# A two-layer decode kernel on one core: hand-written phases against a list scheduler, one pool of ten load slots, a fifth kept V pair and a searched load order

## The chip, the cores and the metric

The kernel runs on one core of a Trainium2 chip. The metric is the device time of one execution in microseconds (us); lower is better. Engines are named as in the profile: PE does matmuls, PEld its weight loads, DVE is the vector engine, ACT does exponentials and copies, SP issues the loads (SPq is its queue). L426 is line 426 of the kernel.

## The reference, cut to what matters

Two layers run one after the other, with the same weights and the same cache. Each is attention of one new token per batch over a cache of 8192 positions, then a gated FFN.

```python
# B=4, Hq=32, Hkv=8, Sk=8192, Dh=128, D=512, F=1792, all bf16
def _A_ref(x, k_cache, v_cache, wq, wo):
    q = (x @ wq) ...                                   # 4 query heads share one K/V head
    scores = einsum("bhqd,bhkd->bhqk", q, k) * Dh ** -0.5
    o = einsum("bhqk,bhkd->bhqd", softmax(scores), v)
    return o ... @ wo

x = x + _A_ref(_layernorm(x), ...)                     # layer 0
x = x + _B_ref(_layernorm(x), ...)                     # silu(x @ w_gate) * (x @ w_up) @ w_down
x = x + _A_ref(_layernorm(x), ...)                     # layer 1: the same K and V again
x = x + _B_ref(_layernorm(x), ...)
```

K and V are 67 MB each, and each layer streams them (the kernel before reads 265.56 MB from HBM for both layers, weights included). One load ("pair") is 1024 KB, called 1 MB here: half the positions of one K or V head. There are 128 K pairs and 128 V pairs in the two layers. A few V pairs of each batch are kept from layer 0 for layer 1 and are loaded only once.

A batch goes from layer 0 to layer 1 alone. In between lies its *chain*: output projection, LayerNorm, FFN, LayerNorm, query projection. The chain is made of many small steps that depend on each other and move no K or V.

## The kernel before: the parts that matter

The order of all work is written by hand as phases. Small steps are put on a list `delayed` and come out one by one after K or V units; at the end of a phase they are all run out (`settle`).

```python
NRING = 10                    # ring of ten 0.5 MB buffers, used strictly in turn
NRET = 8                      # eight 0.5 MB buffers reserved for kept V
TAIL1 = [14, 10, 6]; NFILL = [16, 16, 14, 12]; LATE = [12, 12, 16]; FL = [1, 2, 1, 1, 2, 3, 2, 2]  # tuned by hand
...
def do(u):                    # one K or V unit of 0.5 MB
    if u[0] == "k":
        k_front(u)            # DVE transpose
        ...                   # QK matmuls of the pair before: flush()
    else:
        flush(); v_unit(u)    # 16 P.V matmuls
    run_delayed(); pump()     # small steps; then issue every load whose buffer is free

def settle():
    for _ in range(5):
        run_delayed(True)     # all softmax steps at once, one after the other
...
elif name == "C1":            # the chain of batch b, with FL[i] units between its steps
    hold["on"] = True
    add_to_x(x0T, "x0", OPJ)
    some(FL[0]); ln_center(); some(FL[1]); ffn_gate(); ln_scale()
    ...
```

## Time and profile before

| | before |
|---|---|
| time, median of 3 runs | 704.52 us (703.98 to 706.74) |
| span of the profiled run | 703.3 us |
| read from HBM | 265.56 MB in 240 pair loads and the weights |
| PE, DVE busy | 468.5 us, 380.7 us |

The page of the kernel before, parts 1 to 3: busy time and share of the span, then the DMA engines' busy share in tenths and the GB/s in 40 slices of 17.6 us, then the bytes.

```profile
PE 468.5 (67%) x10564; PEld 275.8 (39%) x10564; DVE 380.7 (54%) x586; ACT 48.6 (7%) x114; POOL 0.7 (0%) x6
...
GB/s 359 375 402 407 285 414 418 420 401 417 412 319 409 420 316 424 397 420 371 360 409 420 397 414 388 410 419 380 301 358 423 410 345 422 386 319 404 404 372 58
...
HBM read 265.56 MB, written 0.00 MB: 378 GB/s over the span
```

No engine is busy all the time. The load stream runs at about 420 GB/s in its good slices (416 to 426 in the undisturbed stretches of 10 us), and dips elsewhere. At 420 GB/s the bytes alone take 265.56 / 0.42 = 632.3 us. The other 71.0 us of the span are start, end and dips. I call this difference, span less bytes at 420 GB/s, the *shortfall*. It is an estimate made from the span and the bytes, and it serves to compare kernels.

The stretches table of the kernel before (stretch in us; length; busy us and count on PE, PEld, DVE, ACT, POOL; granted PE clock; DMA share; GB/s):

```profile
70.00:80.00 10.00, 3.85 (x21) 2.63 (x21) 4.34 (x12) 2.45 (x5) 0.00 (x0) 0.50 0.91 348
80.00:90.00 10.00, 9.26 (x191) 4.02 (x191) 7.06 (x8) 0.00 (x0) 0.00 (x0) 0.50 0.69 247
...
250.00:260.00 10.00, 7.73 (x163) 4.05 (x162) 7.42 (x8) 0.00 (x0) 0.00 (x0) 0.50 0.77 288
...
490.00:500.00 10.00, 5.13 (x147) 4.91 (x147) 1.45 (x9) 0.50 (x2) 0.00 (x0) 0.50 0.82 298
500.00:510.00 10.00, 8.04 (x177) 4.24 (x185) 7.56 (x10) 0.00 (x0) 0.00 (x0) 0.50 0.78 281
```

The dip at 70 to 90 us is the first softmax; 490 to 510 us is a chain. The timeline of DVE at the first softmax of the kernel before (start, length, engine, line, operation, tiles, count; in brackets the idle time before and who ended it, where "issue" means that the engine waited for nothing the profile shows) shows why loading stops:

```profile
62.37 2.37 DVE L412 STREAM_TRANSPOSE ring<-ring 128x1024 uint32<-128x1024 uint32 x2 [0.26 <-DMA ring<-in_A_k_cache_dram]
66.52 2.48 DVE L443 TENSOR_REDUCE negm<-ps 128x1 f32<-128x512 f32 x4 [1.79 <-PE ps L426]
...
72.87 0.24 DVE L500 TENSOR_SCALAR selw<-selL,gl 128x32 f32<-128x32 f32 x1
77.67 0.36 DVE L510 RECIPROCAL invL<-ps 128x32 f32<-128x32 f32 x1 [4.55 <-PE ps L508]
77.94 9.07 DVE L412 STREAM_TRANSPOSE ring<-ring 128x1024 uint32<-128x1024 uint32 x8
```

From 64.7 to 77.9 us DVE transposes no K. In DVE's program the transposes stand behind the last softmax step, for which DVE sits idle 4.55 us; eight follow at once when it is done. No K is consumed, no buffer comes free, and the loading queue stops: in the timeline of SP the load issued at 66.56 us is followed by the next only at 82.31.

```profile
66.56 6.46 SPq L92 DMA_DIRECT2D ring<-in_A_k_cache_dram  x1
82.31 0.33 SPq L92 DMA_DIRECT2D ring<-in_A_v_cache_dram  x1
```

SP's own waits, in total, count and longest, before:

```profile
SPq L62 <- PE ps L426: 329.6, 120, 19.5
SPq L62 <- PE ps L522: 213.1, 89, 11.5
```

L426 are the QK matmuls and L522 the P·V matmuls. SP waits for them because they free the buffers.

### The profile page before, as it was taken

Reading aid. Unit: us, or ns where it says so; the run is one execution under the profiler, and the core shown is the slowest. Engines: PE = TensorE matmul, PEld = TensorE weight load, DVE = VectorE, ACT = ScalarE, POOL = GpSimd, SP = SyncE. Lnnn points to the kernel's source line nnn. Section 1 sums busy time; section 2 is a strip of 40 time slices with the busy share of each in tenths; the row PEclk is TensorE's granted clock in tenths of the full one; section 3 lists DMA queues with packets and bytes.
Section 4 is the critical chain, followed back from the end, with each engine's and each line's share of the span. In section 5 each row is a group of like instructions: output and inputs, shape, how many; then the busy total and the mean of one; then the engine's idle time right before and its main releaser. Section 6 shows DMA issues by size and latency. Waiting matters only on the chain.

```text
span 703.3 us, 22406 instructions
## 1 busy us (share of the span) xinstructions
PE 468.5 (67%) x10564; PEld 275.8 (39%) x10564; DVE 380.7 (54%) x586; ACT 48.6 (7%) x114; POOL 0.7 (0%) x6
## 2 busy tenths in 40 slices
PE   2565656565676577867756678677786676586676
PEld 2111323245642233347522443246432376532375
DVE  4977654540288857741576557652566610289501
ACT  1001100020000110020000200011000110000200
POOL 0000000000000000000000000000000000000000
PEclk9955555555567755555586555655555555567555
DMA  8999799999989989999999999999899999989991
GB/s 359 375 402 407 285 414 418 420 401 417 412 319 409 420 316 424 397 420 371 360 409 420 397 414 388 410 419 380 301 358 423 410 345 422 386 319 404 404 372 58
DMA packets 42268, 267.00 MB, mean 380 GB/s; under 512 B 4024, under 2 KB 9920, under 8 KB 10944
## 3 DMA queue, kind: packets, MB, share of 16 engines
q1 hardware_dynamic: 42176, 265.58, 94.2%
q8 instruction: 82, 1.34, 0.7%
q14 instruction: 10, 0.08, 0.0%
HBM read 265.56 MB, written 0.00 MB: 378 GB/s over the span
## 4 chain that ended last, share of the span: by engine, by line
PE 34%; DMA 31%; DVE 27%; issue 5%; ACT 3%; SPq 1%
DMA ring<-in_A_k_cache_dram 21%; DVE ring L412 21%; PE ps L426 11%; PE ps L522 10%; DMA ring<-in_A_v_cache_dram 8%; DVE negm L443 3%; PE ps L588 3%; PE ps L642 2%; PE ps L489 2%; ACT pp L492 2%; DMA wq_sb<-in_A_wq_dram 2%; PE ps L547 2%; PE ps L678 1%; PE ps L564 1%; DVE pp L480 1%
## 5 line engine op out<-in xcount | busy, mean ns | idle before, releaser
L426 PE MATMUL ps<-ring,qpad 32*32 32x512 bf16 x4096 | 253.5, 566 | 121.3 <-DVE ring L412 120.7
L412 DVE STREAM_TRANSPOSE ring<-ring 128x1024 uint32<-128x1024 uint32 x256 | 299.0, 1217 | 47.9 <-DMA ring<-in_A_k_cache_dram 43.8
L426 PEld LDWEIGHTS ps<-ring,qpad 32*32 32x32 bf16 x4096 | 70.0, 111 | 270.1 <-DVE ring L412 208.7
L522 PE MATMUL ps<-pp,ring 128*128 128x4 bf16 x3072 | 96.3, 166 | 24.3 <-issue 14.3
L522 PEld LDWEIGHTS ps<-pp,ring 128*128 128x128 bf16 x3072 | 92.9, 104 | 44.5 <-issue 32.6
L531 DVE TENSOR_TENSOR oT<-ps,invL 128x4 bf16<-128x4 f32 x64 | 10.7, 167 | 141.0 <-PE ps L522 140.9
L445 ACT ACTIVATE pp<-ps,negm 128x512 bf16<-128x512 f32 x32 | 21.6, 686 | 451.9 <-DVE negm L443 451.9
L522 PE MATMUL ps<-pp,kept 128*128 128x4 bf16 x1024 | 31.8, 166 | 6.9 <-DMA kept<-in_A_v_cache_dram 5.2
L522 PEld LDWEIGHTS ps<-pp,kept 128*128 128x128 bf16 x1024 | 30.1, 104 | 15.4 <-issue 9.6
L443 DVE TENSOR_REDUCE negm<-ps 128x1 f32<-128x512 f32 x32 | 19.9, 682 | 15.1 <-PE ps L426 15.1
L547 PE MATMUL ps<-oT,wo_sb 128*128 128x4 bf16 x640 | 21.5, 166 | 5.0 <-issue 3.3
L588 PE MATMUL ps<-xnT,wq_sb 128*128 128x4 bf16 x640 | 18.7, 166 | 6.8 <-issue 4.5
L489 PE MATMUL ps<-ident,pp 128*128 128x128 bf16 x128 | 16.5, 310 | 9.8 <-ACT pp L492 6.4
L547 PEld LDWEIGHTS ps<-oT,wo_sb 128*128 128x128 bf16 x640 | 20.1, 105 | 6.6 <-issue 4.4
L588 PEld LDWEIGHTS ps<-xnT,wq_sb 128*128 128x128 bf16 x640 | 17.9, 104 | 8.8 <-issue 6.3
L492 ACT ACTIVATE pp<-ps 128x1024 bf16<-128x1024 bf16 x16 | 16.4, 1024 | 32.8 <-PE ps L489 32.8
L463 PE MATMUL ps<-identf,gm 128*1 128x128 f32 x8 | 2.6, 320 | 22.4 <-DVE gm L455 22.4
L489 PEld LDWEIGHTS ps<-ident,pp 128*128 128x128 bf16 x128 | 12.3, 141 | 11.1 <-ACT pp L492 7.4
L567 DVE TENSOR_REDUCE var<-ps 128x4 f32<-128x16 f32 x10 | 1.7, 174 | 25.5 <-PE ps L564 25.5
L580 ACT ACTIVATE lnv<-var,eps_sb 128x4 f32<-128x4 f32 x10 | 3.0, 298 | 153.3 <-DVE var L567 153.3
L510 DVE RECIPROCAL invL<-ps 128x32 f32<-128x32 f32 x8 | 2.9, 357 | 19.1 <-PE ps L508 19.1
L678 PE MATMUL ps<-hT,wd_sb 128*128 128x4 bf16 x280 | 8.5, 166 | 6.0 <-issue 4.7
(68 smaller groups left out, 151.9 us busy)
## 6 DMA issues: line engine op xcount, KB each, us to landing
ring<-in_A_k_cache_dram SPq DMA_DIRECT2D x128, 1024.0 KB, 8.3
ring<-in_A_v_cache_dram SPq DMA_DIRECT2D x96, 1024.0 KB, 9.0
kept<-in_A_v_cache_dram SPq DMA_DIRECT2D x16, 1024.0 KB, 12.8
wq_sb<-in_A_wq_dram SPq DMA_DIRECT2D x1, 4096.0 KB, 12.3
wo_sb<-in_A_wo_dram SPq DMA_DIRECT2D x4, 1024.0 KB, 13.6
wg_sb<-in_B_w_gate_dram SPq DMA_DIRECT2D x2, 896.0 KB, 10.9
wu_sb<-in_B_w_up_dram SPq DMA_DIRECT2D x2, 896.0 KB, 12.2
wd_sb<-in_B_w_down_dram SPq DMA_DIRECT2D x2, 896.0 KB, 15.2
```

What stands on the lines that cost most here:

```text
L412: T.op("dve", lambda e: e.transpose(v, v), reads=[key], writes=[key])
L426: T.op("pe", lambda e: e.matmul(ps[32 * c:32 * (c + 1), a * BW:(a + 1) * BW], lhsT=qp[rows, es_, g, :], rhs=kt[n][rows, :, es_ // 2, :, es ...
L443: T.op("dve", lambda e: e.tensor_reduce(negm[:, q, a:a + 1], bank(a), AX.X, ALU.max, negate=True), reads=[f"pb{a}"], writes=[f"negm{q}_{a}"])
L445: T.op("act", lambda e: e.activation(pblk(q)[:, :, a, :], bank(a).rearrange("p (t j) -> p t j", j=32), ACTF.Exp, bias=negm[:, q, a:a + 1], ...
L489: T.op("pe", lambda e: e.matmul(stg[:, t * P:(t + 1) * P], lhsT=pp[:, q, blk * P:(blk + 1) * P], rhs=ident[:], is_transpose=True, start=Tr ...
L492: T.op("act", lambda e: e.activation(pp[:, q, f * 1024:(f + 1) * 1024], stg[:, :], ACTF.Copy), reads=[f"pb{bk}"], writes=[f"pp{q}_{a}" for ...
L522: T.op("pe", lambda e: e.matmul(ps[:, bk * BW:bk * BW + REP], lhsT=ap[:, t * Dh:(t + 1) * Dh], rhs=pp[:, q, col:col + REP], start=(c == 0 ...
L531: T.op("dve", lambda e: e.tensor_tensor(oT[:, l, g * REP:(g + 1) * REP, b], ps[:, bk * BW:bk * BW + REP], invL[:, q, g * REP:(g + 1) * REP ...
L547: T.op("pe", lambda e: e.matmul(ps[:, OPJ * BW + nq * B:OPJ * BW + (nq + 1) * B], lhsT=wo_sb[:, h, nq * P:(nq + 1) * P], rhs=oT[:, l, h, : ...
L588: T.op("pe", lambda e: e.matmul(misc[:, h * B:(h + 1) * B], lhsT=wq_sb[:, kt, h * Dh:(h + 1) * Dh], rhs=xnT[:, kt * B:(kt + 1) * B], start ...
L642: T.op("pe", lambda e: e.matmul(ps[:, bk * BW + fo * B:bk * BW + (fo + 1) * B], lhsT=w_sb[:, kt, fo * P:(fo + 1) * P], rhs=xnT[:, kt * B:( ...
L678: T.op("pe", lambda e: e.matmul(misc[:, nq * B:(nq + 1) * B], lhsT=wd_sb[:, fo, nq * P:(nq + 1) * P], rhs=hT[:, fo * B:(fo + 1) * B], star ...
```

## The change

The intent: describe the whole program as steps with an engine, a time and dependences; let a list scheduler place all of them and all loads at build time; and issue each engine's instructions in the planned order. The buffers become one pool of ten 1 MB slots, in which kept V simply hold their slot longer. Five pairs per batch are kept instead of eight half pairs (the same as four pairs). The order of the loads is a string found by a search. The step times are written in the code.

```diff
+class Plan:
+    HOP = 0.2
+    LOAD_LEAD = 0.8
+    LOAD_TAIL = 1.4
+    ...
+    def run(self):          # earliest start first; among ready steps, the lowest prio
+        ...
+                    slots.sort()
+                    f, i = slots[0]          # a load takes the slot that comes free first
+        ...
+    def emit(self):
+        for s in sorted(self.steps + self.loads, key=lambda s: (s.start, s.prio[0])):
+            s.fn()
+
+ORDER = ("KKKqKVKKKoKKKgKKKKVKVVKKKgKuKKVoKVVVKKKVKKKVV..."   # cut: K, V pairs and weights
+KEPT = [5, 5, 5, 5]
+NSLOT = 10
...
-        ring = sb("ring", [P, NRING, NB * Dh], BF16)
-        kept = sb("kept", [P, NRET, NB * Dh], BF16)
+        pool = sb("pool", [P, NSLOT, 2 * UE], BF16)
...
+        CHAIN = [-10.0]                       # softmax and chain steps go first when ready
+                tr.append(PL.add("dve", 1.22, t, [ld], prio))            # K transpose
+            st = PL.add("pe", 1.95, qk, tr + [qd, prev] + ..., prio)     # QK of one pair
+                st = PL.add("pe", 1.0, pv, [prev, p_ready[(l, b)], lds.get(u)], prios[i], ...)
+            return PL.add("pe", 0.03 * KT * len(heads), mm, deps, CHAIN, take=tag)   # query projection
...
-        phases = [("A1", 0, A_of(0, 0, range(NCH // 2)))]
-        ...                                   # cut: phases, delayed, settle, hold
+        PL.run()
+        PL.emit()
```

The room for the tenth slot comes mostly from smaller query buffers. Work on the engines is otherwise the same, apart from a query spread of 16 small matmuls where 4 stood.

## The prediction

> **What bounds it now.** The load stream. The page counts 265.6 MB read from HBM in 703.3 us (378 GB/s; load queue 94% of the DMA engines' span). In the table of 10 us stretches the undisturbed ones move 416 to 426 GB/s[...]. At 420 GB/s the bytes take 632 us. Some 2 us at the start and 13 us at the end (after the last P·V matmul: output projection, FFN, store) are without load. So about 55 us are lost in the middle: the stretches at 70-90 us (348, 247 GB/s), 190-210 (341, 325), 240-260 (381, 288), 330-350 (299, 374), 490-520 (298, 281, 360), 560-580, 610-630, 660-670. These are softmaxes and FFN/query chains: nothing is consumed, the ring stays full, and SP's own waits show it (on QK matmuls up to 19.5 us, on P·V up to 11.5 us). The compute engines have room: PE 468 us busy, DVE 381 us.
>
> **What changes.**
> 1. Bytes. 5 kept V pairs of 1 MB per batch instead of 8 half-MB pieces: 236 loads instead of 240, 4.2 MB less, 10 us at 420 GB/s, all critical.
> 2. Buffers. 5 MB ring and 4 MB reserved for kept V become one pool of 10 MB. Kept V come last in each layer-0 V sequence and are read first in layer 1, so part of the time all ten slots are ring: an estimated 25 us of loading ahead instead of 12.5 (2.5 us per MB), 12.5 at worst.
> 3. Order. The chains of small steps get top priority and are interleaved with K and V work by planned times. The table agrees with the trace: transpose 1.22 (trace 1.22), QK pair 1.95 (1.5 to 1.95), P·V pair 1.0 (0.96 to 1.01), gate/up 1.75 (1.65), max 0.7 (0.68), exp 0.9 (0.69+0.21). So in-order queues should seldom be held by a misplaced step. Not in the table: PE's "issue" gaps of 2 to 3.8 us; the deeper pool should absorb them.
> 4. K first, wq fourth: first QK moves from 19 to about 26 us, covered by slots and early transposes. Neutral.
> 5. Unchanged: transposes, QK, P·V, FFN work; the 13 us closing chain; one score buffer, so a softmax still blocks QK for about 4.5 us. Long K runs sit near the DVE limit (2.3 to 2.4 us a pair against 2.5 of loading), so DVE catches up slowly after a softmax.
>
> **Sum.** 704.5 - 10 (bytes) - 27 (half of the 55 us) = about 667 us. Floor by this count: 622 + 15 = 637.
>
> **In the profile after:** HBM read 261.4 MB; mean near 395 GB/s; shorter longest waits of SP; few 10 us stretches below 350; the same end; DVE and PE busy time within 3%; first QK at about 26 us. If 2 is wrong, the dips stay as deep with fewer bytes. If 3 is wrong, DVE or PE idles on a chain step while loaded K or V waits.
>
> **What would make it wrong.** The static order is fragile: a late load or an issue gap holds a whole queue, and loads are bound to a planned release order. Kept V may eat the pool just when a chain needs it. The long K-only and V-only runs in the load order may make a bound of their own (DVE). Better than expected: the dips vanish nearly entirely, 645 to 650.
>
> Chances: faster by over 2% 0.85, within 2% 0.12, slower 0.03. Predicted 667 us, range 647 to 690.

The 4.5 us for which a softmax blocks QK were the author's estimate; in the trace of the kernel before, at the first softmax, 3.7 us pass from the end of the last QK matmul (66.44 us) to the end of the last exp and its sum (70.10).

## The result, and the profile after

| | before | after |
|---|---|---|
| time, median | 704.99 us (4 runs) | 671.44 us (669.65 to 671.93, 4 runs) |
| ratio | 1 | 0.9517 (95%: 0.949 to 0.9544) |
| span of the profiled run | 703.3 us | 670.1 us |
| HBM | 265.56 MB | 261.36 MB |
| bytes at 420 GB/s | 632.3 us | 622.3 us |
| shortfall | 71.0 us | 47.8 us |

A ratio here is the mean time of one kernel's fast runs over that of the other's in the same rounds, so it is not quite the ratio of the medians. The experiments ran in three groups on different chips, so across groups the ratios are compared, not the medians.

The page after:

```profile
PE 459.3 (69%) x10672; PEld 272.4 (41%) x10672; DVE 377.7 (56%) x568; ACT 48.6 (7%) x114; POOL 2.7 (0%) x8
...
GB/s 356 415 399 420 395 419 419 419 418 393 363 416 420 415 408 420 420 420 417 326 423 419 420 398 421 419 420 418 305 422 421 420 420 418 314 402 422 352 375 3
...
HBM read 261.36 MB, written 0.00 MB: 390 GB/s over the span
```

The good slices are no faster than before; there are more of them. The timeline of DVE at the first softmax after:

```profile
75.58 2.45 DVE L574 TENSOR_REDUCE negm<-ps 128x1 f32<-128x512 f32 x4
78.06 0.16 DVE L587 TENSOR_REDUCE gm<-negm 128x1 f32<-128x4 f32 x1
78.13 1.23 DVE L544 STREAM_TRANSPOSE pool<-pool 128x1024 uint32<-128x1024 uint32 x1
79.29 0.64 DVE L600 TENSOR_REDUCE rowm<-ps 1x128 f32<-1x512 f32 x1
79.86 1.22 DVE L544 STREAM_TRANSPOSE pool<-pool 128x1024 uint32<-128x1024 uint32 x1
```

While one softmax step is away on PE or ACT, DVE transposes K. The dip of the first softmax is gone: the stretches 70 to 90 us move 393 and 402 GB/s. What is left stands at the chains and at the last softmax, at 630 us (stretches table, after; columns as before; the first two lines are the first softmax):

```profile
70.00:80.00 10.00, 4.24 (x56) 1.07 (x63) 9.05 (x12) 2.79 (x8) 0.00 (x0) 0.50 1.04 393
80.00:90.00 10.00, 8.29 (x127) 3.52 (x118) 8.23 (x15) 2.34 (x3) 0.00 (x0) 0.67 1.03 402
...
320.00:330.00 10.00, 7.68 (x227) 5.02 (x224) 5.54 (x9) 0.00 (x0) 0.00 (x0) 0.58 0.78 293
...
470.00:480.00 10.00, 7.62 (x229) 5.51 (x227) 7.56 (x13) 0.50 (x2) 0.00 (x0) 0.50 0.69 268
...
580.00:590.00 10.00, 9.05 (x268) 5.53 (x264) 5.93 (x12) 0.00 (x0) 0.00 (x0) 0.61 0.78 289
...
630.00:640.00 10.00, 8.05 (x228) 7.66 (x229) 1.20 (x7) 2.05 (x2) 0.00 (x0) 0.50 0.75 286
```

SP's own waits, after (L556 is QK, L694 is P·V):

```profile
SPq L62 <- PE ps L556: 282.6, 115, 8.7
SPq L62 <- PE ps L694: 191.9, 97, 12.3
```

The longest wait behind QK fell from 19.5 to 8.7 us. That behind P·V did not fall.

### The profile page after: what moved, and what is told of

Its sections match the earlier page's. It is cut to its first block, busy times and chain, and to the rows that moved or that the text cites. A ratio compares the mean times of both kernels' runs of the same rounds, so it can differ in the third digit from the quotient of the medians.

```text
span 670.1 us, 22609 instructions
## 1 busy us (share of the span) xinstructions
PE 459.3 (69%) x10672; PEld 272.4 (41%) x10672; DVE 377.7 (56%) x568; ACT 48.6 (7%) x114; POOL 2.7 (0%) x8
## 3 DMA queue, kind: packets, MB, share of 16 engines
q8 instruction: 83, 1.36, 0.8%
HBM read 261.36 MB, written 0.00 MB: 390 GB/s over the span
## 4 chain that ended last, share of the span: by engine, by line
DMA 65%; PE 20%; DVE 9%; issue 4%; SPq 1%; ACT 1%; DVEq 0%
DMA pool<-in_A_k_cache_dram 33%; DMA pool<-in_A_v_cache_dram 32%; PE ps L694 7%; PE ps L556 7%; DVE pool L544 6%; PE ps L433 2%; DVE negm L574 1%; SPq L92 1%; PE ps L632 1%; PE ps L672 1%; PE ps L721 1%; ACT pp L638 1%; PE ps L395 1%; PE ps L763 0%; DVE pp L623 0%
## 5 line engine op out<-in xcount | busy, mean ns | idle before, releaser
L544 DVE STREAM_TRANSPOSE pool<-pool 128x1024 uint32<-128x1024 uint32 x256 | 304.5, 1224 | 122.5 <-DMA pool<-in_A_k_cache_dram 117.0
L556 PE MATMUL ps<-pool,qpad 32*32 32x512 bf16 x4096 | 245.7, 571 | 77.4 <-DVE pool L544 72.1
L694 PE MATMUL ps<-pp,pool 128*128 128x4 bf16 x4096 | 125.1, 166 | 70.2 <-DMA pool<-in_A_v_cache_dram 51.3
L694 PEld LDWEIGHTS ps<-pp,pool 128*128 128x128 bf16 x4096 | 117.4, 104 | 105.9 <-DMA pool<-in_A_v_cache_dram 78.2
L556 PEld LDWEIGHTS ps<-pool,qpad 32*32 32x32 bf16 x4096 | 68.4, 113 | 207.2 <-DVE pool L544 133.7
L672 PEld LDWEIGHTS ps<-oT,wo_sb 128*128 128x128 bf16 x640 | 20.6, 104 | 20.4 <-issue 11.9
L721 PE MATMUL ps<-xnT,wu_sb 128*128 128x4 bf16 x280 | 8.2, 166 | 2.8 <-DVE oT L707 1.4
L623 DVE TENSOR_SCALAR pp<-pp,alpha 128x512 bf16<-128x512 bf16 x32 | 9.0, 343 | 1.8 <-ACT alpha L616 1.8
L763 PEld LDWEIGHTS ps<-hT,wd_sb 128*128 128x128 bf16 x280 | 7.9, 104 | 3.7 <-issue 3.0
L721 PEld LDWEIGHTS ps<-xnT,wu_sb 128*128 128x128 bf16 x280 | 7.9, 104 | 3.1 <-issue 1.6
L721 PEld LDWEIGHTS ps<-xnT,wg_sb 128*128 128x128 bf16 x280 | 8.8, 107 | 0.0
## 6 DMA issues: line engine op xcount, KB each, us to landing
wg_sb<-in_B_w_gate_dram SPq DMA_DIRECT2D x2, 896.0 KB, 19.5
```

What stands on the lines that cost most here:

```text
L544: op("dve", lambda e: e.transpose(v, v), reads=[key], writes=[key])
L556: op("pe", lambda e: e.matmul(ps[32 * c:32 * (c + 1), a * BW:(a + 1) * BW], lhsT=qpad[rows, qbuf, es_, g, :], rhs=ap[h][rows, :, es_ // 2, ...
L672: op("pe", lambda e: e.matmul(ps[:, OPJ * BW + nq * B:OPJ * BW + (nq + 1) * B], lhsT=wo_sb[:, h, nq * P:(nq + 1) * P], rhs=oT[:, l, h, :], ...
L694: op("pe", lambda e: e.matmul(ps[:, bk * BW:bk * BW + REP], lhsT=ap[:, t * Dh:(t + 1) * Dh], rhs=pp[:, q, col:col + REP], start=(i == 0 an ...
L721: op("pe", lambda e: e.matmul(ps[:, bk * BW + fo * B:bk * BW + (fo + 1) * B], lhsT=w_sb[:, kt, fo * P:(fo + 1) * P], rhs=xnT[:, kt * B:(kt ...
L763: op("pe", lambda e: e.matmul(ps[:, bk * BW + nq * B:bk * BW + (nq + 1) * B], lhsT=wd_sb[:, fo, nq * P:(nq + 1) * P], rhs=hT[:, fo * B:(fo ...
```

## The experiments

Question one was what gained the 33 us: the bytes, the slots, the sharing of slots, the placing of steps, or the searched order. My theory was the sum of the prediction: 10 us of bytes, the rest from the deeper pool and from placing. The main rival was that the searched load order did it.

### Only the scheduler, on nine slots, with the old load order

```diff
-NSLOT = 10
+NSLOT = 9
-KEPT = [5, 5, 5, 5]
+KEPT = [4, 4, 4, 4]
-ORDER = (...)                 # searched
+ORDER = (...)                 # the 240 loads in the order of the kernel before
-        vgroups = [(0, 0, g) for g in v_first(0)] ...
+        vgroups = [...]       # the V groups in the order of the kernel before
```

> The kernel after, with the load order, V group order, kept set (4 MB a batch, 240 loads) and total buffer (nine 1 MB slots) of the kernel before: only the list scheduler and the sharing of the slots are new. Theory A (the 23 us beyond the bytes come from steps placed by planned times and shared slots): 685 to 692 us. Rival B (they come from the searched load order, and the scheduler only serves it): 698 to 706 us, as before.

Measured: 686.0 us, ratio 0.9749 (0.9716 to 0.9782). The load order, the kept set, the bytes and the buffer space are the old ones, and 2.5% is gained. The rival falls as the main cause.

### The same, with the kept slots reserved again

```diff
-        slots = [(0.0, i) for i in range(self.nslots)]
+        pools = [[(0.0, i) for i in range(5)], [(0.0, i) for i in range(5, self.nslots)]]
+        # layer-0 loads of kept V use the second list, all other loads the first
```

> The nine-slot version with the old load order (686.0 us), but four of its slots reserved for kept V and five for all else, as before: only the placing of steps, and the free choice among the five, are left of the change. If placing the steps is what gained 18.6 us: within 3 us of 686. If sharing the slots did: 698 to 706 us, as before.

Measured: 687.45 us, ratio 0.9728 (0.968 to 0.9775), the same as with sharing. So with nine slots and this order, sharing brings nothing that can be measured; 2.7%, about 19 us, come from the rest of the rewrite: the placing of steps, and with it the free choice among the five slots, which the old ring took strictly in turn. Those two were not separated further, nor was a third thing that every run with the scheduler has: it chooses the PSUM bank of each small step, where the old code fixed it. The trace does show placing at work: with the old order and the reserved slots, this run moves 401 and 417 GB/s at 70 to 90 us, where the kernel before moves 348 and 247.

### The tenth slot

```diff
-NSLOT = 9
+NSLOT = 10                    # still the old load order, 240 loads
```

> The same with ten slots. Theory A with the pool size as a large part: 8 to 12 us under the nine-slot version, about 680. Rival B: within 3 us of the nine-slot version.

Measured: 677.53 us, ratio 0.9626 (0.9594 to 0.9658). The tenth slot is worth 1.2%, about 9 us.

### The searched order with the old kept set

```diff
-KEPT = [5, 5, 5, 5]
+KEPT = [4, 4, 4, 4]
-        nk = -(-KEPT[b] // NCP)
+        nk = 3                # the V groups keep their order
+# ORDER: four more V, each just before its group's second pair
```

> The kernel after with four kept V pairs per batch (the set kept before), so 240 loads; the four more loads stand in the order just before their group's second pair. If the bytes count in full: 10 us slower, 681 us. If fewer kept V free slots just when a chain needs them, the dips shrink and it gives part back: 674 to 678 us.

Measured: 673.05 us, ratio 0.9563 (0.9527 to 0.9599), just under the second range. Against the old order on ten slots the searched order gives 0.6%; the intervals touch. Against the kernel after it loses 1.6 us by the medians and 0.5%, or 3.2 us, by the ratios, and the intervals overlap, so that loss is not clear of noise. The 10 us that the bytes should cost are not there. The page says where they went, in the lines of this run:

```profile
span 671.2 us, 22618 instructions
...
GB/s 356 415 401 418 396 417 419 418 418 395 399 416 418 421 419 419 419 420 411 343 416 419 420 418 420 419 419 419 349 419 420 419 418 420 390 342 423 418 395 7
...
HBM read 265.56 MB, written 0.00 MB: 396 GB/s over the span
```

It moves 4.2 MB more, at 396 GB/s instead of 390. Its shortfall is 671.2 - 632.3 = 38.9 us against 47.8 us. Some dips are shallower: 399 for 363 in slice 11 and 349 for 305 in slice 29, both at chains, and 418 for 352 in slice 38, at the last softmax. Slices 35 and 36, at the fourth chain, read 390 and 342 for 314 and 402: that dip has mostly moved. In longer stretches around the chains (165 to 205, 310 to 350, 465 to 505 and 565 to 615 us of both traces) loading falls short of 420 GB/s by 11.6 us in all, against 15.6 us in the kernel after; from 625 to 645 us, at the last softmax, by 0.3 against 3.3 us. So the fifth kept pair saves 10.0 us of loading, and 8.9 us come back as waiting, most of it at these places. One slot less is held by kept V there. That this slot is the reason is argued and not shown: no run kept five pairs with an eleventh slot.

### The searched order on nine slots

```diff
-NSLOT = 10
+NSLOT = 9                     # all else as after
```

> The kernel after with nine slots in place of ten, order and kept set as they are (236 loads). If the tenth slot is what rides out the chains: 6 to 12 us slower than the kernel after, 678 to 683 us. If order and scheduling do it: within 3 us, 671 to 674 us.

Measured: 710.62 us (707.06 to 714.86), ratio 1.0098 (1.0047 to 1.015): 1% slower than the kernel before. I expected at most 12 us and got 39. The old order loses about 9 us without the tenth slot; the searched order, with five kept pairs, loses four times that. The rate over the span falls to 367 GB/s. Which of the two, the order or the fifth kept pair, makes it so brittle was not separated.

### A scheduler with wrong times

```diff
-        self.eng, self.us, ... = eng, us, fn, prio
+        self.eng, self.us, ... = eng, us if eng == "sp" or us < 0.1 else 1.0, fn, prio
```

> The kernel after, but the scheduler believes that every step on PE, DVE and ACT takes 1 us (load times kept). If the true step times are what makes the placement good: slower by 10 us or more, over 681. If any dependency-respecting interleaving with chains first does: within 4 us of 671.

Measured: 690.75 us, ratio 0.9778 (0.9733 to 0.9822), 2.7% slower than with the true table, as the first theory expected. Dependences are still kept and chain steps still go first when ready. The loss stands at the chains: in the four long stretches named above loading falls short by 35.1 us instead of 15.6. The first softmax does without the true times: 70 to 90 us still move 392 and 402 GB/s. A rival stands untested: the load order was searched against the true table, and nine_slots shows how badly this order bears another plan. Part of the 2.7% may be that mismatch and not the step times themselves; an old order with a flat table was not run.

### What is left: the chains, and what makes them long

Question two was why dips remain at the chains. The timeline of PE in the chain at 455 to 477 us of the kernel after (idle time before a group in brackets):

```profile
460.93 0.46 PE L763 MATMUL ps<-hT,wd_sb 128*128 128x4 bf16 x12
463.33 1.33 PE L763 MATMUL ps<-hT,wd_sb 128*128 128x4 bf16 x44 [1.95 <-issue]
464.53 0.99 PE L694 MATMUL ps<-pp,pool 128*128 128x4 bf16 x32
465.38 0.59 PE L395 MATMUL ps<-XT,onesm 128*128 128x16 f32 x2
465.81 1.47 PE L694 MATMUL ps<-pp,pool 128*128 128x4 bf16 x50
469.55 0.53 PE L694 MATMUL ps<-pp,pool 128*128 128x4 bf16 x14 [2.26 <-issue]
469.94 0.59 PE L395 MATMUL ps<-sqT,onesm 128*128 128x16 f32 x2
470.36 3.13 PE L433 MATMUL ps<-xnT,wq_sb 128*128 128x4 bf16 x112
```

Count the matmuls between the gaps: 44 + 32 + 2 + 50 = 128, and 14 + 2 + 112 = 128, after which the next gap of 2.27 us comes. The page counts as many weight loads as matmuls (10672 each), so 128 matmuls stand for 256 instructions of PE and PEld. The page's part 3 has a queue of their own for instructions:

```profile
q8 instruction: 83, 1.36, 0.8%
```

These are 83 packets of 16 KB (1.36 MB), one per 128 of PE's 10672 matmuls. Their records in the trace stand at the gaps:

```
instruction packet      PE idle            packet ends   PE resumes    later by
460.99 to 462.05 us     461.4 to 463.33    462.05        463.33        1.28 us
467.14 to 468.24        467.3 to 469.55    468.24        469.55        1.31
473.22 to 474.33        473.5 to 475.76    474.33        475.76        1.43
```

The count follows the matmuls in other runs too: the kernel before, with 10564 matmuls, has 82 packets, and pad_instr below, with 512 more than the kernel after, has 87. In dense stretches the packets follow each other every 6.0 to 6.5 us where the load queue is full (6.15 between the first two above; 461 to 473 us move 417 GB/s), every 5.4 to 5.5 us at the fourth chain (568.6 to 579.5 us, 379 to 381 GB/s), and every 3.6 to 3.9 us where it runs dry or has (294 to 323 GB/s over such an interval at the chains, 4 GB/s from 655.8 to 659.6 us). PE needs about 3.5 us for 128 small matmuls (112 took 3.13 us, 27 ns from one to the next), so with the load queue full it waits in each block: the gaps in the dense stretches of the kernel after are 1.9 to 2.8 us. The packets at 438.11, 447.44, 454.51 and 460.99 us lie 9.3, 7.1 and 6.5 us apart, and PE waits 1.95 us at the last one all the same.

To test it, two kernels put the same PE time into the four chains, once in many instructions and once in few.

```diff
 # pad_instr: the query projections of a chain are issued twice
-                for h in heads:
+                for h in (list(heads) * 2 if len(heads) < Hq else heads):
```

> The kernel after with every query projection of the four chains issued twice (128 more small matmuls a chain, about 3.4 us of PE at the 27 ns that they take; same result). Theory F (the dips left are chains slowed by PE's instruction supply, 128 matmuls per 6.15 us while the load queue is full): each chain 6 us longer, and 15 to 25 us more in all. Rival (PE work or latency bounds the chains): as pad_time, within 3 us.

```diff
 # pad_time: four wide dummy matmuls ahead of each half, overwritten afterwards
+                for _ in range(4 if len(heads) < Hq else 0):
+                    op("pe", lambda e: e.matmul(bank(bk), lhsT=ident[:], rhs=wq_sb[:, 0, 0:BW], start=True, stop=True), ...)
```

> The kernel after with 8 dummy matmuls of 512 columns ahead of the query projections of each chain: about 3.4 us of PE as in pad_instr, but 8 instructions pairs in place of 128. Theory F: 5 to 14 us over the kernel after, and 6 us or more under pad_instr. Rival: equal to pad_instr within 3 us.

Measured, on the same chip: 689.62 us (ratio 0.9771) and 676.28 us (ratio 0.9584). The timelines of PE at the third chain, pad_instr first:

```profile
479.47 3.13 PE L433 MATMUL ps<-xnT,wq_sb 128*128 128x4 bf16 x112
484.85 3.58 PE L433 MATMUL ps<-xnT,wq_sb 128*128 128x4 bf16 x128 [2.26 <-issue]
488.86 0.59 PE L433 MATMUL ps<-xnT,wq_sb 128*128 128x4 bf16 x16 [0.43 <-issue]
489.38 0.68 PE L446 MATMUL ps<-qT,ident 128*32 128x16 bf16 x32
490.01 5.44 PE L556 MATMUL ps<-pool,qpad 32*32 32x512 bf16 x96
```

and pad_time:

```profile
473.03 1.49 PE L432 MATMUL ps<-wq_sb,ident 128*128 128x512 bf16 x3 [0.22 <-issue]
474.31 1.89 PE L436 MATMUL ps<-xnT,wq_sb 128*128 128x4 bf16 x64
476.44 1.49 PE L432 MATMUL ps<-wq_sb,ident 128*128 128x512 bf16 x3 [0.24 <-issue]
477.72 1.89 PE L436 MATMUL ps<-xnT,wq_sb 128*128 128x4 bf16 x64
479.55 0.68 PE L449 MATMUL ps<-qT,ident 128*32 128x16 bf16 x32
480.18 4.60 PE L559 MATMUL ps<-pool,qpad 32*32 32x512 bf16 x96
```

The first is within its range. The second is 4.7 us by the ratios, just under the range of 5 to 14, and 13 us under pad_instr, so the rival falls. From the start of the query projection to the first QK matmul the four chains take 6.80, 6.95, 6.55 and 5.56 us in the kernel after; 12.38, 11.26, 10.54 and 9.24 in pad_instr; 7.15, 7.89, 7.15 and 7.89 in pad_time (starts read from the traces). The sums are 25.9, 43.4 and 30.1 us, so the chains grew by 17.5 and 4.2 us. Of each four dummies only three are in the trace; taken from the LayerNorm matmul just before (L395), which all three traces have, the growths are 17.6 and 5.8 us. By the ratios the times grew by 17.9 and 4.7 us, give or take some 4 us (an estimate from their intervals). In the four long stretches named above loading falls short by 33.2 and 22.3 us, against 15.6. Two things follow. A microsecond of chain costs about a microsecond of time: the chains are on the critical path. And wide matmuls are cheap where PE waited for a block anyway (the gap of 2.27 us is gone in pad_time): they lengthen the first three chains by 0.7 to 1.3 us. The fourth chain, whose gap was only 0.55 us, grew by 2.7. Small matmuls cost their full time and, where the load queue is full, a wait on top (2.26 us ahead of the 128 more in the chain shown). Per chain, 128 small matmuls, about 3.5 us of PE, cost 4.4 us, and 8 wide ones of nearly the same PE time about 1.4 us (5.8 by four). My expectation of 6 us per chain in pad_instr was too high: 4.4 us was measured, since in three of the four chains the last gap is only 0.2 to 0.7 us (0.43 in the one shown): there the load queue has run dry (213 GB/s at 480 to 490 us of that run).

### Three attempts to use it, and a control

The scheduler knows nothing of instruction blocks. I gave it a rule: a block of 128 matmuls is there no sooner than 6.15 us after PE entered the block before it.

```diff
+            while s.n - k >= left_in[0]:      # s.n matmuls in this PE step
+                k += left_in[0]
+                t = max(at + s.us * k / s.n, ready[0])
+                at = t - s.us * k / s.n
+                s.end = at + s.us
+                ready[0] = t + 6.15
+                left_in[0] = 128
+            left_in[0] -= s.n - k
```

> The kernel after, with one rule more in the scheduler: PE gets its instructions in blocks of 128 matmuls, and a block is there no sooner than 6.15 us after PE entered the one before it (the trace's figure under a full load queue). Load order and kept set unchanged. Theory F: planned and real order agree better around the chains, 666 to 671 us. If the order of loads, made for the old plan, is what binds: 670 to 674, no gain.

Measured: 675.03 us, ratio 0.9556 (0.9524 to 0.9588). The kernel after has 0.9517 (0.949 to 0.9544); the intervals overlap. So the rule alone is no gain and at most a small loss, and both expected ranges missed.

With the rule, I searched load order, kept counts and group cuts again:

> The same rule, and the load order, kept counts (2, 5, 4, 2) and group cuts searched anew against it. Theory F: faster than the kernel after by 5 to 12 us, 659 to 667 us. If the rule misses what the chip does: 670 us or more.

> A second end of that search, kept counts (2, 4, 3, 3), another load order. Theory F expects 660 to 668 us, within 3 us of fetch_search; a lone lucky order would show as a difference over 5 us.

Measured: 675.87 us (ratio 0.957) and 678.49 us (ratio 0.9609). Both missed the times that Theory F expected; that they lie within 3 us of each other held. The page of the first shows what changed:

```profile
span 674.1 us, 22627 instructions
...
HBM read 268.70 MB, written 0.00 MB: 399 GB/s over the span
```

This is fetch_search. Its shortfall is 674.1 - 268.70 / 0.42 = 34.3 us, against 47.8 us of the kernel after: the shortfall did go down, by 13.5 us. But the search kept fewer V pairs, (2, 5, 4, 2) instead of 5 each, and the 7.3 MB more cost 17.5 us at 420 GB/s. My reading, which no run tests: the rule prices a stall too high, since it charges 6.15 us even where the load queue has run dry and blocks come every 3.6 us, and so the search bought stalls off with bytes at a loss. A rule that depends on the load queue was not tried.

The control: the same search for the same time, against the scheduler as it is.

> Control: the same search for the same time, against the scheduler as it is, without the rule; kept counts stay 5. If searching longer is what helps: 664 to 668 us. Theory F: no gain, 669 to 674 us.

Measured: 670.17 us, ratio 0.9494 (0.9463 to 0.9525); its interval overlaps that of the kernel after, as Theory F expected. More search against the old plan brings nothing that is clear of noise. No version here clearly beats the change.

### The runs together

The shortfall is that of the one profiled run; for nine_slots it was the slowest of four (714.86 us).

| run | us, median | ratio to before | MB | shortfall, us |
|---|---|---|---|---|
| before | 704.99 | 1 | 265.56 | 71.0 |
| split_pool: steps placed by the scheduler | 687.45 | 0.9728 | 265.56 | 53.6 |
| old_order_9: slots shared too | 686.00 | 0.9749 | 265.56 | 53.7 |
| old_order_10: tenth slot | 677.53 | 0.9626 | 265.56 | 42.4 |
| kept_four: searched order | 673.05 | 0.9563 | 265.56 | 38.9 |
| after: fifth kept pair | 671.44 | 0.9517 | 261.36 | 47.8 |
| nine_slots | 710.62 | 1.0098 | 261.36 | 90.8 |
| table_flat | 690.75 | 0.9778 | 261.36 | 65.1 |
| pad_instr | 689.62 | 0.9771 | 261.36 | 65.2 |
| pad_time | 676.28 | 0.9584 | 261.36 | 52.0 |
| fetch_plan | 675.03 | 0.9556 | 261.36 | 50.9 |
| fetch_search | 675.87 | 0.9570 | 268.70 | 34.3 |
| fetch_search_b | 678.49 | 0.9609 | 269.75 | 33.8 |
| blind_search | 670.17 | 0.9494 | 261.36 | 47.0 |

## Why the prediction was right, point by point

The total was right: 671.4 us against 667 predicted, in a range of 647 to 690. The two terms of the sum were both off, in opposite directions. That the total came out within 5 us of the prediction is therefore partly luck.

1. *What bounds the kernel* was right. Load stream, dips at softmaxes and chains: the placing of steps took the dip of the first softmax away (split_pool shows it alone), and the pads show that chain time is paid about in full.
2. *"4.2 MB less, 10 us at 420 GB/s, all critical"* is the term that failed. The bytes fell as computed, but the time by 1.6 to 3.2 us, not clear of noise. The shortfall rose from 38.9 to 47.8 us. The fifth kept pair holds a slot at chains and softmaxes; that this is the reason is argued. The prediction named this danger ("Kept V may eat the pool just when a chain needs it") and yet put the 10 us in the sum in full.
3. *"27 (half of the 55 us)"* was mis-sized the other way. With the old bytes the change of scheduler, slots and order gives 704.6 - 673.05 = 31.5 us in the first group of runs. By the ladder of ratios it is 2.5 to 2.7% for placing the steps (with the free choice of slots and banks), 1.2% for the tenth slot and 0.6% for the searched order.
4. *Buffers.* The mechanism was right where it says that more room helps (9 us for the tenth slot), and not shown where it says sharing: split_pool and old_order_9 are equal.
5. *"The deeper pool should absorb"* the issue gaps: wrong. They lie on PE in the chains, make the chains longer, and chain time is paid in full.
6. *In the profile after:* 261.36 MB for 261.4; 390 GB/s for about 395; DVE and PE busy within 3% (377.7 for 380.7 and 459.3 for 468.5); first QK at 27.7 us for about 26 (in the kernel before at 20.6, not 19); the end after the last P·V matmul 11.1 us (659.0 to 670.1), where the prediction had 13 and the kernel before has 11.5; the longest wait of SP behind QK more than halved, that behind P·V unchanged; inside the span four 10 us stretches under 350 GB/s (three at chains, one at the last softmax). All but the wait behind P·V came about nearly as said. That K first is neutral was not tested.
7. *The table of step times is good:* with the searched order a flat table costs 2.7%, at the chains. The prediction rested on this and planned no run to test it.

## What to carry to other kernels

Even when the load stream bounds the kernel, a saved load can earn less than its bytes, here 1.6 to 3.2 us for 10: compare the bytes saved with the loading ahead that is given up. A static schedule made from measured step times can be worth more than buffers or fewer bytes, because it puts long work into the waits of short dependent steps: here DVE's K transposes of 1.2 us stand between the steps of the first softmax, where the kernel before let DVE sit idle for 4.55 us at once. But an order searched for one buffer count should be tuned again when the count changes: here one slot less turned a gain of 4.8% into a loss of 1.0%.
